# Spreading four rows of reciprocals over partitions 0, 4, 8 and 12, in an attention and MLP kernel with a planned order

## The chip, the cores and the metric

The kernel runs on one core of one Trainium2 chip. Times are device microseconds (us) of one execution; the time before is the median of three runs, 830.73 us (829.04 to 832.25). The profile is of one further execution.

A core has five engines with instruction queues of their own, which meet only through semaphores: TensorE (PE) multiplies matrices into PSUM, VectorE (DVE), ScalarE (ACT) and GpSimd (POOL) work on elements, and SyncE (SP) issues the DMA copies. Each engine takes its instructions strictly in the order in which they were written for it. Data lie in SBUF, 128 partitions wide.

## The reference

One input x of 2048 rows by 640 is normalised by row (layernorm without weights). Two branches share the result, and both are added to x:

```python
x = A_x
xn = _layernorm(x, axis=-1)
return x + _A_ref(xn, A_wq, A_wk, A_wv, A_wo) + _B_ref(xn, B_w1, B_w2)
```

Branch A is attention with 32 query heads of 20 features and a single key and value head: q = xn wq, k = xn wk, v = xn wv, softmax over 2048 keys of the scaled scores, times v, and the heads joined times wo. Branch B is silu(xn w1) w2 with 1728 hidden features. All is bf16 in and out.

## The kernel before, in words

**Tiling.** The 2048 query rows are cut in 4 chunks of 512 (QC, QW), the 32 heads in 8 groups of 4 (NG, HG), each head in a slot of 32 partitions (SLOT). That makes 32 groups (chunk, head group), in order. A group goes over 16 key tiles of 128 keys. For each key tile and head, PE makes scores of 128 keys by 512 queries in a PSUM bank (`s_mm`, line 758). Most go to ACT, two or three heads at a time, for the exponential (line 793). The others are key tiles that the planner gives to DVE, which builds the exponential of all four heads from integer and multiply steps (line 936, then 957, 959 and 961). PE then multiplies by v (lines 822 and, for the tiles of DVE, 1137) and accumulates one PSUM bank for the four heads. Row 20 of each head's slot holds the sum of the exponentials, the softmax denominator.

**End of a group.** `end_group` (line 857) copies the bank to `U_sb` (line 863). For chunks 0 to 2, which have 24 of the 32 groups, `norm_job` (line 579) then makes a chain with four SP steps:

- la (line 585): a DMA copies the four rows of denominators, 512 values each, into a [128, 16] tile.
- recip (line 588): DVE takes the reciprocals.
- lb (line 590): a DMA copies them back as four rows of 512 fp32 values to `Rrow`, which lies in partitions 0 to 3 of the middle third of `nblk`.
- lc (line 592): four DMAs, one for each head; each reads one row of `Rrow` 32 times and writes it to the 32 partitions of that head's slot in `Rrep`, 64 KB.
- normalisation (line 595): POOL multiplies `U_sb` by `Rrep` into `oU`; it waits for the four lc copies.
- packs (line 606): four or five DMAs put the heads' 20 rows each in their place in `oT`, the transposed attention output.

The last chunk normalises in another way (`ut_job`, with PE transposes).

**Other work of PE.** Between the attention steps PE projects q (line 502), makes the hidden layer (line 522, with its activation on ACT, line 528, and DVE, line 531) and the output. An output job (`out_job`, line 623) of a chunk makes 128 rows by 320 columns in one PSUM bank: 14 matmuls of branch B (`ffn_mms`, line 556) and then 5 of branch A (`o_mms`, line 561, matmul on line 565), which read `oT` and so wait for all packs of that chunk. DVE adds x (line 635), SP stores (line 620).

**What sets the order.** A planner in Python (`Sched`, `build`) runs through the program once with an estimated duration for each operation and writes one list for each engine; `emit` (line 1306) turns the dependences into semaphore waits. The chip's true times change no order. At each step the planner picks, for the engine that is free first, an operation whose estimated start is near; PE chooses among scores, PV, the current other job and DVE's key tiles. A job of the other work, once begun, is finished before the next begins (`cur_job`, line 1158), and holds one of the two spare banks (`XBANKS`, line 33 and following; DVE's key tiles use them too). For an SP operation the planner counts 600 ns of SP time and a single common DMA stream, whose time for a copy is its stated number of bytes over 250 per ns (lines 303 and 304):

```python
op = Op("sp", fn, 600.0, nbytes / 250.0, pre=pre, reads=reads, writes=writes, prio=prio, name=f"dma {key}")
```

and when the operation is put in the list (lines 204 and 205):

```python
self.dma_free = max(self.dma_free, start + 1300.0) + op.lat
op.fin = self.dma_free + 700.0
```

The stated bytes of an lc copy are `2 * SLOT * QW * 4` = 131,072, twice the 64 KB that it moves.

Of the kernel before, what the change touches and what calls it, by code (L numbers as in the profile page):

```python
# [13 lines left out]
P = 128  # L14
# [4 lines left out]
SLOT = 32  # L19
HG = 4  # L20
NG = H // HG
QW = 512
# [197 lines left out]
def build(nc, A_x, A_wq, A_wk, A_wv, A_wo, B_x, B_w1, B_w2, out, stack):  # L220
# [11 lines left out]
    def sb(shape, dt):  # L232
        cnt[0] += 1
        return stack.enter_context(nc.sbuf_tensor(f"sbt{cnt[0]}", shape, dt))

    def sem(name):
        return stack.enter_context(nc.semaphore(name))
# [27 lines left out]
    rLg = sb([P, 2, HG * QW // P], F32)  # L265
    nblk = sb([P, 3 * QW], F32)
    Rrep = nblk[:, 0:QW]
    Rrow = nblk[0:HG, QW:2 * QW]
    oU = nblk[:, 2 * QW:3 * QW].bitcast(BF16).rearrange("p (u q) -> p u q", u=2)
    o_norm = nblk[:, 0:QTP * D // 2].bitcast(BF16).rearrange("p (t d) -> p t d", t=QTP)  # L270
    t_buf = sb([P, 2, QW], BF16)
# [24 lines left out]
    def res(*k):  # L296
        if k not in R:
            R[k] = Res()
        return R[k]
# [3 lines left out]
    def dma(key, fn, nbytes, reads=(), writes=(), pre=(), prio=0.0):  # L303
        op = Op("sp", fn, 600.0, nbytes / 250.0, pre=pre, reads=reads, writes=writes, prio=prio, name=f"dma {key}")
        if key not in dma_sems:
            dma_sems[key] = [sem(f"d_{key}"), 0]
        op.dma_sem = key
        return sc.add(op)

    def dve(fn, occ, lat=65.0, **kw):  # L310
        return sc.add(Op("dve", fn, occ, lat, **kw))
# [4 lines left out]
    def pool(fn, occ, lat=60.0, **kw):  # L316
        return sc.add(Op("pool", fn, occ, lat, **kw))
# [21 lines left out]
    def load_x(n):  # L339
# [9 lines left out]
         reads=[res("idf")], writes=[res("idf")], prio=0.02)  # L349
    pool(lambda g: g.memset(mhalf[:, :], -0.5), 120, writes=[res("mh")], prio=0.03)  # L350
    idb = pool(lambda g: g.tensor_copy(ident_b[:, :], ident_f[:, :]), 290, reads=[res("idf")], writes=[res("idb")],
               prio=0.04)
    pool(lambda g: g.memset(wv_sb[:, :, :], 0.0), 180, writes=[res("wv")], prio=0.05)
    for n in range(4):
# [3 lines left out]
        writes=[res("wqp")], prio=0.06)  # L358
    vms = pool(lambda g: g.memset(v_all[:, :, :, :], 0.0), 900, writes=[res("v")], prio=0.6)
    v1s = []  # L360
    for j, cj in enumerate((1.0, C_W)):
        v1s.append(pool(lambda g, j=j, cj=cj: g.memset(v_all[:, j, :, DH:DH + 1], 0.5 * cj), 120,
                        pre=[vms], writes=[res("v")], prio=0.6 + 0.01 * j))

    def wrow(ap):
# [4 lines left out]
                writes=[res("wqs0")])  # L370
    wk_cp = [pool(lambda g, r=r: g.tensor_copy(wk_sb[:, :, r * SLOT:r * SLOT + DH], wk_sb[:, :, 0:DH]), 240, pre=[d_wk],
                  reads=[res("wk")], writes=[res("wkr", r)], prio=0.08) for r in range(1, HG)]
    for n in range(4, 8):
# [3 lines left out]
               writes=[res("wqs")])  # L377
# [3 lines left out]
    def wq_dst(c):  # L381
# [5 lines left out]
        reads=[res("wqs0")], pre=[pool_wq0, d_wq0], writes=[res("wqp0")], prio=0.15)  # L387
    wqp_op = []
    for c in range(DC):
        wqp_op.append(pool(lambda g, c=c: g.tensor_copy(  # L390
            wq_dst(c)[:, HG:H, 0:DH], wq_st[:, c, HG * DH:D].rearrange("p (h j) -> p h j", j=DH)), 640,
            reads=[res("wqs")], pre=[pool_wq0, d_wq], writes=[res("wqp", c)], prio=0.7))
# [181 lines left out]
    def oT_free(qc):  # L574
        return qc < 2 or all((qc - 2, i) in out_done for i in range(QTP))
# [3 lines left out]
    def norm_job(g, uc):  # L579

        qc, gi = divmod(g, NG)
        us, par = g % 2, qc % 2
        u0 = U_sb[DH:DH + 1, us, :]
        pu = u0.ap[0][0]
        la = dma(f"la{us}", lambda e: e.dma_start(
            Lg[:, us, :], bass.AP(U_sb, u0.offset, [[pu * SLOT, HG], [HG * QW // P, SLOT], [1, HG * QW // P]])), 8192,
            pre=[uc], reads=[res("U", us)], writes=[res("Lg", us)], prio=0.5)
        rc = dve(lambda v: v.reciprocal(rLg[:, us, :], Lg[:, us, :]), 230, pre=[la], reads=[res("Lg", us)],
                 writes=[res("rLg", us)], prio=0.1, name="recip")
        lb = dma(f"lb{us}", lambda e: e.dma_start(Rrow.rearrange("h (j e) -> h j e", j=SLOT), rLg[:, us, :]),  # L590
                 8192, pre=[rc], reads=[res("rLg", us)], writes=[res("Rrow")], prio=0.5)
        lc = [dma(f"lc{us}", lambda e, h=h: e.dma_start(Rrep[h * SLOT:(h + 1) * SLOT, :],
                                                        bass.AP(nblk, Rrow[h:h + 1, :].offset, [[Rrow.ap[0][0], 1], [0, SLOT], [1, QW]])),
                  2 * SLOT * QW * 4, pre=[lb], reads=[res("Rrow")], writes=[res("Rrep", h)], prio=0.5) for h in range(HG)]
        nm = pool(lambda e: e.tensor_tensor(oU[:, us, :], U_sb[:, us, :], Rrep, ALU.mult), 1300, pre=[uc] + lc,  # L595
                  reads=[res("U", us)] + [res("Rrep", h) for h in range(HG)], writes=[res("oU", us)], prio=0.1)
        un_op[(qc, gi)] = nm
        packs = []
        for i in range(HG):
            row = (gi * HG + i) * DH  # L600
            lo = i * SLOT
            left = DH
            while left:
                c, r = divmod(row, P)
                n = min(left, P - r)
                o = dma(f"pk{us}", lambda e, c=c, r=r, n=n, lo=lo: e.dma_start(oT[r:r + n, par, c, :], oU[lo:lo + n, us, :]),  # L606
                        n * QW * 2, pre=[nm], reads=[res("oU", us)], writes=[res("oT", par, gi, i, c)], prio=0.6)
                o.gate = lambda: oT_free(qc)
                packs.append(o)
                row, lo, left = row + n, lo + n, left - n  # L610
        pack_op[(qc, gi)] = packs
# [245 lines left out]
    def end_group(g, pv):  # L857
        us = g % 2

        def com(op):  # L860
            att["pgroup"] = g + 1
        up = [un_op[((g - 2) // NG, (g - 2) % NG)]] if g >= 2 else []
        uc = Op("dve", lambda v: v.tensor_copy(U_sb[:, us, :], bk(UB)), t_dve(512), 65, pre=[pv] + up, reads=[sc.banks[UB]],  # L863
                writes=[res("U", us)], prio=-1.0, on_commit=com, name=f"Ucopy{g}")
        sc.add(uc)
        qc = g // NG
        if qc < QC - 1:
            norm_job(g, uc)
        else:
            misc_front.append(ut_job(qc, g % NG, uc, us))  # L870
        if g == NGR - 1:
            for i in range(QTP):
                misc_front.append(("oT", qc, i))
            if qc == QC - 1:
                for i in range(QTP):
                    for hf in range(2):
                        misc_front.append(("fin", qc, i, hf))
# [391 lines left out]
    while not finished():  # L1269
# [7 lines left out]
        e = min(sc.ENG, key=lambda k: sc.t[k])  # L1277
# [127 lines left out]
def bass_kernel(nc, A_x, A_wq, A_wk, A_wv, A_wo, B_x, B_w1, B_w2, out):  # L1405
    with ExitStack() as stack:
        XB_EXTRA[:] = [b for buf in ABUFS for b in buf]
        sc, dma_sems, sem = build(nc, A_x, A_wq, A_wk, A_wv, A_wo, B_x, B_w1, B_w2, out, stack)
        run = emit(nc, sc, dma_sems, sem)
        with nc.Block() as block:  # L1410
            @block.sync
            def _(e):
                run("sp", e)

            @block.gpsimd
            def _(e):
                run("pool", e)

            @block.vector
            def _(e):  # L1420
                run("dve", e)

            @block.scalar
            def _(e):
                run("act", e)

            @block.tensor
            def _(e):
                run("pe", e)
# [34 lines left out]
```

## Time and profile before

| what | value |
|---|---|
| median of 3 runs | 830.73 us |
| the profiled execution | 830.86 us |
| its span, first to last instruction | 829.1 us |
| granted TensorE clock, mean | 0.971 |
| lc copies (line 592) | 96, 64.0 KB each, median 6.5 us from issue to landing |
| lb copies (line 590) | 24, from 57.1 to 627.7 us |
| normalisations on POOL (line 595) | 24, median 1276 ns, the first at 70.5, the last at 641.5 us |
| packs (line 606) | 108, median 716 ns of SP's time each |
| exponentials on ACT (line 793) | 651 instructions, 754.9 us busy |
| key tiles on DVE (line 961) | 105 |

How to read it: busy time of an engine is the sum of its instructions. "Idle, released by" names what an engine waited for. A landing is the time from a DMA's issue to the arrival of its last byte's semaphore. The chain is followed back from the last instruction, at each step to what released it. The clock is the one that PE was granted, as a share of full speed.

### The profile page before, as it was taken

Reading aid. Unit: us, or ns where it says so; the run is one execution under the profiler, and the core shown is the slowest. Engines: PE = TensorE matmul, PEld = TensorE weight load, DVE = VectorE, ACT = ScalarE, POOL = GpSimd, SP = SyncE. Lnnn points to the kernel's source line nnn. Section 1 sums busy time; section 2 is a strip of 40 time slices with the busy share of each in tenths; the row PEclk is TensorE's granted clock in tenths of the full one; section 3 lists DMA queues with packets and bytes.
Section 4 is the critical chain, followed back from the end, with each engine's and each line's share of the span. In section 5 each row is a group of like instructions: output and inputs, shape, how many; then the busy total and the mean of one; then the engine's idle time right before and its main releaser. Section 6 shows DMA issues by size and latency. Waiting matters only on the chain.

```text
span 829.1 us, 15373 instructions
## 1 busy us (share of the span) xinstructions
PE 734.0 (89%) x6578; PEld 237.8 (29%) x6578; DVE 665.3 (80%) x1023; ACT 771.0 (93%) x715; POOL 57.3 (7%) x64
## 2 busy tenths in 40 slices
PE   7899999988977999888896999989898799999986
PEld 5322222222222332222222333322222233333323
DVE  8468688888875897899886889899888588888773
ACT  3899999999996999999996999999999699999992
POOL 7400000000000000000000000000000000000000
PEclk9899999999997999999998999999999899999998
DMA  8403432324440444542334433433344000010000
GB/s 269 155 4 15 18 13 15 16 14 19 16 17 13 27 26 17 57 18 13 15 16 17 22 17 24 63 17 16 17 16 18 13 9 17 1 33 2 1 1 32
DMA packets 26044, 22.96 MB, mean 28 GB/s; under 512 B 11704, under 2 KB 22264, under 8 KB 25976
## 3 DMA queue, kind: packets, MB, share of 16 engines
q1 hardware_dynamic: 25976, 21.99, 30.0%
q8 instruction: 51, 0.84, 0.4%
q14 instruction: 17, 0.14, 0.1%
HBM read 10.70 MB, written 2.62 MB: 16 GB/s over the span
## 4 chain that ended last, share of the span: by engine, by line
ACT 78%; PE 10%; issue 4%; DVE 3%; DMA 2%; SPq 1%; POOL 1%; POOLq 0%
ACT sbt L793 75%; PE psall L758 3%; ACT sbt L528 3%; PE psall L556 2%; PE psall L822 2%; PE psall L565 1%; DMA sbt<-sbt 1%; DVE sbt L936 1%; SPq L606 1%; PE psall L522 1%; DMA sbt<-in_A_wq_dram 1%; PE psall L459 0%; PE psall L433 0%; DMA sbt<-in_A_wk_dram 0%; POOL sbt L595 0%
## 5 line engine op out<-in xcount | busy, mean ns | idle before, releaser
L793 ACT ACTIVATE sbt<-psall 128x1536 bf16<-128x1536 f32 (+1 forms) x651 | 754.9, 1366 | 29.5 <-PE psall L758 29.1
L936 DVE TENSOR_SCALAR sbt<-psall 128x512 int16<-128x512 f32 x420 | 282.7, 686 | 85.5 <-PE psall L758 80.9
L758 PE MATMUL psall<-sbt 32*128 32x512 bf16 x2048 | 284.4, 389 | 61.4 <-ACT sbt L793 50.4
L822 PE MATMUL psall<-sbt 128*32 128x512 bf16 x2468 | 207.0, 390 | 2.8 <-ACT sbt L793 1.5
L758 PEld LDWEIGHTS psall<-sbt 32*128 32x128 bf16 x2048 | 71.0, 91 | 296.1 <-ACT sbt L793 246.8
L961 DVE TENSOR_TENSOR sbt<-sbt 128x2048 bf16<-128x2048 bf16 x105 | 132.9, 1265 | 1.4
L556 PE MATMUL psall<-sbt 128*128 128x320 bf16 x448 | 85.5, 304 | 0.3 <-DVE sbt L936 0.2
L522 PE MATMUL psall<-sbt 128*128 128x512 bf16 (+1 forms) x280 | 81.6, 388 | 2.5 <-DVE sbt L936 1.4
L822 PEld LDWEIGHTS psall<-sbt 128*32 128x32 bf16 x2468 | 51.5, 94 | 108.5 <-issue 84.8
L959 DVE TENSOR_SCALAR sbt<-sbt 128x2048 int16<-128x2048 int16 x105 | 75.0, 715 | 1.3
L957 DVE TENSOR_SCALAR sbt<-sbt 128x2048 int16<-128x2048 int16 x105 | 73.3, 698 | 3.0 <-PE psall L822 1.4
L595 POOL TENSOR_TENSOR sbt<-sbt 128x512 bf16<-128x512 f32 x24 | 33.6, 1399 | 577.1 <-DVE sbt L936 214.9
L1137 PE MATMUL psall<-sbt 128*32 128x512 bf16 (+1 forms) x752 | 55.1, 383 | 1.2 <-DVE sbt L344 1.2
L556 PEld LDWEIGHTS psall<-sbt 128*128 128x128 bf16 x448 | 36.1, 98 | 45.0 <-issue 29.6
L565 PE MATMUL psall<-sbt 128*128 128x320 bf16 x160 | 33.0, 329 | 18.0 <-DMA sbt<-sbt 18.0
L531 DVE SCALAR_TENSOR_TENSOR sbt<-sbt,psall 128x512 bf16<-128x512 bf16 (+1 forms) x56 | 38.2, 682 | 13.0 <-ACT sbt L528 8.9
L502 PE MATMUL psall<-sbt 128*128 128x512 bf16 (+1 forms) x175 | 47.9, 370 | 0.5 <-DVE sbt L936 0.3
L528 ACT ACTIVATE sbt<-psall 128x512 bf16<-128x512 f32 (+1 forms) x56 | 43.5, 776 | 0.6 <-PE psall L522 0.6
L522 PEld LDWEIGHTS psall<-sbt 128*128 128x128 bf16 (+1 forms) x280 | 21.0, 99 | 42.2 <-issue 21.7
L863 DVE COPY sbt<-psall 128x512 f32<-128x512 f32 x32 | 21.9, 684 | 12.1 <-PE psall L822 12.0
L506 DVE TENSOR_SCALAR sbt<-psall 128x512 bf16<-128x512 f32 x32 | 21.9, 685 | 4.5 <-PE psall L502 4.0
L1137 PEld LDWEIGHTS psall<-sbt 128*32 128x32 bf16 x752 | 18.8, 102 | 19.5 <-issue 11.2
(49 smaller groups left out, 166.5 us busy)
## 6 DMA issues: line engine op xcount, KB each, us to landing
sbt<-sbt SPq DMA_DIRECT2D x96, 64.0 KB, 6.5
sbt<-in_A_x_dram SPq DMA_DIRECT2D x28, 160.0 KB, 2.9
out_dram<-sbt SPq DMA_DIRECT2D x16, 160.0 KB, 1.9
sbt<-in_B_w_dram SPq DMA_DIRECT2D x1, 2160.0 KB, 11.0
sbt<-in_B_w_dram SPq DMA_DIRECT2D x1, 2080.0 KB, 15.8
sbt<-sbt SPq DMA_DIRECT2D x84, 20.0 KB
sbt<-sbt SPq DMA_DIRECT2D x54, 8.0 KB
sbt<-in_A_wo_dram SPq DMA_DIRECT2D x1, 800.0 KB, 17.6
```

The costliest lines, as they stand in the source:

```text
L502: return pe.matmul(bk(b, lo, hi), wq_pad[:, c, g * P:(g + 1) * P], xnT[:, c, qc * QW + lo:qc * QW + hi], start=(c == 0), stop=(c == DC - 1))
L522: return pe.matmul(bk(b, 0, QW, rows=rows), w1_sb[:, c, fk * P:fk * P + rows], xnT[:, c, qc * QW:(qc + 1) * QW], start=(c == 0), stop=(c = ...
L528: t = Op("act", lambda a: a.activation(t_buf[0:rows, ts, :], bk(job.bank, 0, QW, rows=rows), AF.Tanh, scale=0.5), t_act(512), 95, pre=[job ...
L556: return pe.matmul(bk(b, 0, e1 - e0), hT[par][0:rows, fk, i * P:(i + 1) * P], w2_sb[0:rows, fk, e0:e1], start=(start and fk == 0), stop=(s ...
L758: return pe.matmul(bk(b), kT_rep[i * SLOT:(i + 1) * SLOT, kt * P:(kt + 1) * P], qT[i * SLOT:(i + 1) * SLOT, g % NQ, :], start=True, stop=T ...
L793: return a.activation(Ebuf[:, es, 0:w], ps[:, buf[0] * BANK:buf[0] * BANK + w], AF.Exp, scale=ESCALE)
L822: ins = pe.matmul(ps[i * SLOT:(i + 1) * SLOT, UB * BANK:UB * BANK + QW], lhsT, rhs, start=(first and k < HG), stop=(last and k >= len(lst) ...
L936: p1 = Op("dve", lambda v: v.tensor_scalar(z16[:, i * QW:(i + 1) * QW], bk(job.bank), ZBIAS, 0.0, ALU.add, ALU.max), t_dve(QW), 65, pre=[o ...
L957: m = dve(lambda v: v.tensor_scalar(m_t[:, :].bitcast(I16), z16, 0x7F, 0x3F80, ALU.bitwise_and, ALU.bitwise_or), t_dve(N, 4), pre=st["p1"] ...
L959: wop = dve(lambda v: v.tensor_scalar(w[:, :].bitcast(I16), z16, 0x7F80, None, ALU.bitwise_and), t_dve(N, 4), pre=[m], reads=zr, writes=[r ...
L961: zm = dve(lambda v: v.tensor_tensor(z[:, :], z[:, :], m_t[:, :], ALU.mult), t_dve(N, 2), pre=[wop], reads=zr + [res("m")], writes=zr, pri ...
L1137: ins = pe.matmul(ps[i * SLOT:(i + 1) * SLOT, UB * BANK:UB * BANK + n], zero_t[:, 0:SLOT], zero_t[:, 0:n], start=fresh, stop=fresh, tile_p ...
```

## The change

`Rrow` becomes a view of 16 partitions, of which rows 0, 4, 8 and 12 are used: lb writes its four rows there, and lc reads row 4h for head h. The stated bytes of each lc copy, which only the planner uses, go from 2 to 3 times `SLOT * QW * 4`. The number of DMAs, what they move and where it ends up in `Rrep` stay the same. The planner makes the whole order of all engines anew with the new number.

```diff
-    Rrow = nblk[0:HG, QW:2 * QW]
+    Rrow = nblk[0:4 * HG, QW:2 * QW]
...
-        lb = dma(f"lb{us}", lambda e: e.dma_start(Rrow.rearrange("h (j e) -> h j e", j=SLOT), rLg[:, us, :]),
+        lb = dma(f"lb{us}", lambda e: e.dma_start(
+            bass.AP(nblk, Rrow.offset, [[4 * Rrow.ap[0][0], HG], [HG * QW // P, SLOT], [1, HG * QW // P]]), rLg[:, us, :]),
                  8192, pre=[rc], reads=[res("rLg", us)], writes=[res("Rrow")], prio=0.5)
         lc = [dma(f"lc{us}", lambda e, h=h: e.dma_start(Rrep[h * SLOT:(h + 1) * SLOT, :],
-                                                        bass.AP(nblk, Rrow[h:h + 1, :].offset, [[Rrow.ap[0][0], 1], [0, SLOT], [1, QW]])),
-                  2 * SLOT * QW * 4, pre=[lb], reads=[res("Rrow")], writes=[res("Rrep", h)], prio=0.5) for h in range(HG)]
+                                                        bass.AP(nblk, Rrow[4 * h:4 * h + 1, :].offset, [[Rrow.ap[0][0], 1], [0, SLOT], [1, QW]])),
+                  3 * SLOT * QW * 4, pre=[lb], reads=[res("Rrow")], writes=[res("Rrep", h)], prio=0.5) for h in range(HG)]
```

## The prediction

> **What bounds the kernel now.** I read the page's busy times first, then the waits, then ACT's busy time by stretches, then the chain at the places where ACT stands still, and last the DMA traffic just ahead of them.
>
> ```profile
> PE 734.0 (89%) x6578; PEld 237.8 (29%) x6578; DVE 665.3 (80%) x1023; ACT 771.0 (93%) x715; POOL 57.3 (7%) x64
> ```
>
> ACT works 771.0 of 829.1 us, nearly all of it exponentials (line 793). Three stretches that leave out the prologue and three short places, by columns length, PE, PEld, DVE, ACT, POOL, clock, DMA share and GB/s:
>
> ```profile
> 60.00:246.00 186.00, 168.26 (x1428) 47.85 (x1424) 156.70 (x228) 185.22 (x181) 9.41 (x7) 0.99 0.37 16
> 463.00:640.00 177.00, 161.80 (x1476) 49.64 (x1479) 154.65 (x226) 176.67 (x165) 10.15 (x7) 1.00 0.42 24
> 657.40:814.00 156.60, 142.99 (x1328) 48.37 (x1326) 124.50 (x188) 155.48 (x137) 0.00 (x0) 0.99 0.03 10
> ```
>
> ACT is at 99% there. Inside these stretches only less work for ACT can help. Its idle time lies at the start and at three places, which the waits name:
>
> ```profile
> PE psall L565 <- DMA sbt<-sbt: 18.0, 3, 6.7
> ACT sbt L793 <- PE psall L758: 29.1, 19, 6.8
> ```
>
> PE stops three times, for 18.0 us together, at the o_mms matmuls (line 565) behind a DMA between SBUF addresses; ACT's longest waits for PE are at the same places. The chain at the first of them (start, length, what):
>
> ```profile
> 247.80 1.27 POOL sbt L595
> 249.09 0.80 SPq L606
> ...
> 251.47 1.90 DMA sbt<-sbt
> 253.37 0.05 issue
> 253.41 0.45 PE psall L565
> ```
>
> The normalisation of the last head group of a q chunk (POOL, line 595) starts at 247.80, four pack copies (line 606) follow, the last lands at 253.37, and PE, idle for 6.71 us since 246.70, goes on. At the other two places PE waits 5.92 us (to 452.92) and 5.41 us (to 647.16). Why does POOL start so late? It waits for the four row copies of line 592. The DMA traffic from 629 to 643 us, ahead of the third stall, in 40 slices:
>
> ```profile
> DMA  2000019999399399939939595971966111000000
> GB/s 23 0 0 0 0 12 47 41 35 29 12 35 35 12 35 29 29 12 35 35 12 47 18 29 18 47 23 6 47 23 23 29 18 47 0 0 0 0 0 0
> ```
>
> And line 592 in the group ahead of the first stall:
>
> ```profile
> DMA to landing us min/median/max: 4.6/7.3/9.3
> ```
>
> Four copies are issued within about 2.5 us (there at 236.53, 237.13, 237.77 and 238.40; ahead of the third stall from 629.84), yet traffic runs on from 631 to 641 at some 27 GB/s (4 x 64 KB in 9.7 us), with the DMA engines marked busy. The first copy lands 4.6 us after its issue, the last 9.3 us after, at 238.40 + 9.3 = 247.70; POOL starts at 247.80. So these copies go through one after the other, and they set the start of the normalisation.
>
> **The price of one stall** is more than PE's wait. The granted clock after the first stall is 0.50 until 259, and ACT idles again:
>
> ```profile
> 246.70:253.40 6.70, 0.01 (x2) 0.00 (x0) 0.00 (x0) 1.06 (x2) 1.26 (x1) 0.66 0.07 13
> 253.40:255.00 1.60, 1.59 (x8) 0.65 (x9) 0.52 (x1) 0.55 (x1) 0.00 (x0) 0.50 0.00 0
> 255.00:257.00 2.00, 2.00 (x10) 0.34 (x8) 0.67 (x2) 1.73 (x2) 0.00 (x0) 0.50 0.03 8
> 257.00:259.00 2.00, 2.00 (x9) 0.39 (x7) 0.31 (x1) 0.54 (x2) 0.00 (x0) 0.50 0.00 0
> ```
>
> From ACT's timeline: first stall 6.69 + 0.27 + 1.47 + 0.16 = 8.6 us of idle ACT; second 6.8; third 5.28 + 1.25 = 6.5. Together **21.9 us**. That is all there is to gain here.
>
> **The change, part by part.**
>
> *Number of instructions.* 24 groups, each with 1 copy lb, 4 copies lc, 1 normalisation, 4 or 5 packs, as before; SP's issue time of about 0.6 us for each stays. Nothing on PE, ACT or DVE is added. Cost 0.
>
> *lb to partitions 0, 4, 8, 12.* Same bytes in the same 64-byte pieces. From the issue of lb (234.46) to the first lc (236.53) it takes 2.07 us now; its traffic is a small part of that, so I give it 0 (at most 0.2 us either way, ten per cent of the step).
>
> *lc from four rows farther apart.* No row of this trace shows two copies from rows four partitions apart. Bounds: at worst the four still go in sequence, as now, and nothing is gained; a loss I exclude, because each copy still moves the same 32 pieces of 2 KB out of one partition. At best each lands as the first one does, 4.6 us after its issue: the last gains 9.3 - 4.6 = 4.7 us. Two rows decide between these. The output stores, which read 128 partitions of SBUF, land 160 KB in a median 1.9 us, while the row copies need a median 6.5 us for 64 KB: the engines are not what limits, the source rows are. And the first copy shows what one row alone costs. I take the near side of the best end, **4.4 us**, since each copy uses the same 16 engines and can't quite ignore its neighbours: the traffic of one copy is a quarter of 9.7, so 2.4 us; the fourth starts 1.9 us (238.40 - 236.53) after the first and ends no earlier than 1.9 + 2.4 = 4.3 us into the traffic; some 0.9 us of queueing on top makes 5.3 in place of 9.7.
>
> [...]
>
> *The planner's cost, 2 to 3 units.* In line 304 a copy then counts 196,608/250 = 786 ns in place of 524. With SP's 600 ns spacing and lines 204 and 205, the last of four ends 4324 ns after the first's start now, and 5146 ns after. So in the plan, normalisation and packs come 0.82 us later, and the planner has 0.82 us more time to put other PE work ahead of the o_mms. On the chip that is worth up to 0.8 us at each of the three places. I take 0.8; bounds 0 and about 1.1 (one round of scores and PV more, e.g. 0.61 + 0.40 us).
>
> *At the 21 other groups* the normalisation comes 4.4 us sooner, too; PE never waited for those packs, SP only holds its queue less long for line 595 (225.6 us over 24 groups). Worth 0. The out job holds one of two spare banks 0.8 us longer in the plan, one 0.69 us step of DVE (line 936) at each of three places; I count it within the range.
>
> *The sum.* Sooner and later together 4.4 + 0.8 = 5.2 us at each stall. PE's waits become 6.71 - 5.2 = 1.5, 5.92 - 5.2 = 0.7 and 5.41 - 5.2 = 0.2. ACT's idle time then is about 2.4 us, plus 1.0 us for some lowered clock after the longest: 3.4 in place of 21.9. **Gain 18.5 us.** What follows each stall is ACT at 99%, so it passes to the end whole. The profiled execution took 830.86 us (span 829.1 and 1.8 around it), 0.13 over the median 830.73. 830.86 - 18.5 = 812.4. What is late next is ACT itself.
>
> **The new order.** From the first out job on (246 of 829 us) the planner's times differ, so all it decides later may differ. Price: one key tile (four heads) that moves from DVE to ACT costs 4 x 754.9/1628 = 1.86 us of ACT (651 instructions, 326 of three tiles and 325 of two). There are 105 such tiles on DVE. I allow 4 of them either way, +-7 us.
>
> **Rivals.**
> 1. *Half the overlap*: the engines take copies partly in turn, and the last lands only 2 us sooner. PE's waits become 3.9, 3.1 and 2.6, the lowered clock stays in part (2 us in all). Gain 21.9 - 9.6 - 2 = 10 us: about 820. For it: all copies use the same engines.
> 2. *Still in sequence*: the move does nothing, the plan's 0.8 us at three places remains: 830.9 - 2.4 = 828.5. For it: 27 GB/s is also what engines in turn would show. Against it: stores of 160 KB in 1.9 us.
> 3. *Slower*: the new plan gives DVE fewer key tiles, in the part behind the first out job, because its spare banks are held longer; at 1.86 us for a tile it decides from 10 tiles (18.5 us) on, and from 13 the kernel is slower by over 0.5%: 835 or more. Against it: only three holds of 0.8 us change in the plan. For it: a greedy plan can turn on small times.
>
> **How the numbers follow.** Forecast 0.68, its own range 803 to 820; half the overlap 0.14 (816 to 824); still in sequence 0.10 (825 to 832); slower 0.08 (835 to 845). The range for 8 in 10 takes the forecast and nearly all of the half: 803 to 825. A measurement of this kernel can tell about 0.5% (4.2 us) from no change. Faster by more than that (under 826.6): 0.68 + 0.14 + a fifth of the sequence = 0.84; within it 0.08; slower 0.08.
>
> **What would show it.** Right: the four lc copies land 4.5 to 5.5 us after their issue, all alike; GB/s above 27 in bursts of some 5 us; PE's wait at line 565 for DMA under 4 us in all; no clock of 0.50 behind it; ACT at 95% or more. Wrong: landing still 9 us for the last (rival 2); or landing as forecast and ACT's count of exponentials risen from 651, its busy time well over 771 us (rival 3); or a new wait of PE in place of line 565.

## The result, and the profile after

The changed kernel takes 810.56 us (median of 4 runs, 807.85 to 810.83) against 831.49 us (4 runs, 829.04 to 836.88) for the kernel before, measured together: a ratio of 0.9732, 95% interval 0.968 to 0.9785. Forecast were 812.4 us and a range of 803 to 825. The profiled execution took 810.33 us with a span of 808.5 us; the one before 830.86 and 829.1.

In the changed file everything after line 590 stands one line lower: the exponential is line 794, the score matmul 759, PV 823, the row copies 593, POOL's normalisation 596, the packs 607. Busy times, waits, and the landing of all 96 row copies (least, median, longest) in the changed kernel:

```profile
PE 717.0 (89%) x6501; PEld 235.2 (29%) x6554; DVE 668.3 (83%) x1030; ACT 769.5 (95%) x714; POOL 58.1 (7%) x64
```

```profile
PE psall L565 <- DMA sbt<-sbt: 1.5, 2, 1.1
...
ACT sbt L794 <- PE psall L759: 11.9, 17, 1.8
```

```profile
DMA to landing us min/median/max: 3.5/3.8/4.8
```

ACT's work is nearly the same (771.0 before). What shrank is its idle time, 829.1 - 771.0 = 58.1 us before and 808.5 - 769.5 = 39.0 after. PE's waits for a DMA at line 565 fell from 18.0 to 1.5 us. The row copies land after 3.5 to 4.8 us, where it was 4.5 to 9.8. The traffic ahead of the first output job (229 to 243 us, 40 slices):

```profile
DMA  0000000100000001110001999709979671100000
GB/s 0 0 0 0 0 0 0 17 6 0 0 0 0 0 0 47 10 13 0 0 0 12 47 41 35 29 35 117 129 70 117 53 35 6 18 6 0 0 0 0
```

The same 256 KB that took some 10 us at 27 GB/s now pass in about 5 us, with slices above 100 GB/s. On the chain of waits in that place POOL starts at 241.80, and PE's matmul follows the last pack:

```profile
241.80 1.35 POOL sbt L596
...
243.17 0.79 SPq L607
...
245.54 1.90 DMA sbt<-sbt
...
247.49 1.25 PE psall L565 x4
```

From the issue of the first row copy to POOL's start it is 241.80 - 235.45 = 6.35 us; before, 247.80 - 236.53 = 11.27. The four copies of this group land 3.7 to 4.4 us after their issue, where it was 4.6 to 9.3.

### The profile page after: what moved, and what is told of

Same layout as the page of the kernel before. It is cut to its first block, busy times and chain, and to the rows that moved or that the text cites. A ratio compares the mean times of both kernels' runs of the same rounds, so it can differ in the third digit from the quotient of the medians.

```text
span 808.5 us, 15272 instructions
## 1 busy us (share of the span) xinstructions
PE 717.0 (89%) x6501; PEld 235.2 (29%) x6554; DVE 668.3 (83%) x1030; ACT 769.5 (95%) x714; POOL 58.1 (7%) x64
## 4 chain that ended last, share of the span: by engine, by line
ACT 80%; PE 13%; DVE 4%; DMA 1%; SPq 1%; issue 1%; POOL 0%; ACTq 0%
ACT sbt L794 76%; PE psall L759 4%; ACT sbt L528 3%; PE psall L556 3%; PE psall L823 2%; PE psall L565 1%; DVE sbt L937 1%; DVE sbt L960 1%; PE psall L502 1%; DMA sbt<-in_A_x_dram 1%; SPq L607 1%; DMA sbt<-sbt 0%; DVE sbt L962 0%; PE psall L459 0%; POOL sbt L596 0%
## 5 line engine op out<-in xcount | busy, mean ns | idle before, releaser
L794 ACT ACTIVATE sbt<-psall 128x1536 bf16<-128x1536 f32 (+2 forms) x650 | 754.9, 1365 | 12.6 <-PE psall L759 11.9
L937 DVE TENSOR_SCALAR sbt<-psall 128x512 int16<-128x512 f32 x424 | 286.0, 685 | 77.8 <-PE psall L759 73.6
L962 DVE TENSOR_TENSOR sbt<-sbt 128x2048 bf16<-128x2048 bf16 x106 | 129.6, 1223 | 1.2
L960 DVE TENSOR_SCALAR sbt<-sbt 128x2048 int16<-128x2048 int16 x106 | 78.3, 739 | 1.1
L958 DVE TENSOR_SCALAR sbt<-sbt 128x2048 int16<-128x2048 int16 x106 | 74.6, 703 | 3.4 <-PE psall L823 1.4
L522 PE MATMUL psall<-sbt 128*128 128x512 bf16 (+1 forms) x252 | 73.6, 383 | 4.0 <-issue 1.6
L1138 PE MATMUL psall<-sbt 128*32 128x512 bf16 (+1 forms) x724 | 53.4, 377 | 1.5 <-DVE sbt L344 1.2
L502 PE MATMUL psall<-sbt 128*128 128x512 bf16 (+1 forms) x153 | 41.0, 367 | 2.2 <-issue 1.3
L864 DVE COPY sbt<-psall 128x512 f32<-128x512 f32 x32 | 21.9, 686 | 10.4 <-PE psall L823 10.3
```

The source lines that it names most:

```text
L502: return pe.matmul(bk(b, lo, hi), wq_pad[:, c, g * P:(g + 1) * P], xnT[:, c, qc * QW + lo:qc * QW + hi], start=(c == 0), stop=(c == DC - 1))
L522: return pe.matmul(bk(b, 0, QW, rows=rows), w1_sb[:, c, fk * P:fk * P + rows], xnT[:, c, qc * QW:(qc + 1) * QW], start=(c == 0), stop=(c = ...
L794: return a.activation(Ebuf[:, es, 0:w], ps[:, buf[0] * BANK:buf[0] * BANK + w], AF.Exp, scale=ESCALE)
L937: p1 = Op("dve", lambda v: v.tensor_scalar(z16[:, i * QW:(i + 1) * QW], bk(job.bank), ZBIAS, 0.0, ALU.add, ALU.max), t_dve(QW), 65, pre=[o ...
L958: m = dve(lambda v: v.tensor_scalar(m_t[:, :].bitcast(I16), z16, 0x7F, 0x3F80, ALU.bitwise_and, ALU.bitwise_or), t_dve(N, 4), pre=st["p1"] ...
L960: wop = dve(lambda v: v.tensor_scalar(w[:, :].bitcast(I16), z16, 0x7F80, None, ALU.bitwise_and), t_dve(N, 4), pre=[m], reads=zr, writes=[r ...
```

## The experiments

Two things were changed at once: the place of the rows and the planner's count. Theory: the place makes the copies land sooner, PE's three waits at line 565 shrink, ACT goes on. Rivals: the new order of the engines is the cause; the copies still hinder each other by engine and not by place. All ratios are to the kernel before on the same chip, run beside each group of experiments (medians 832.20, 831.23 and 832.75 us on the three chips used), so they, and not the medians of different chips, are to be compared.

**The place alone.**

```diff
-                  3 * SLOT * QW * 4, pre=[lb], reads=[res("Rrow")], writes=[res("Rrep", h)], prio=0.5) for h in range(HG)]
+                  2 * SLOT * QW * 4, pre=[lb], reads=[res("Rrow")], writes=[res("Rrep", h)], prio=0.5) for h in range(HG)]
```

> Rows in partitions 0, 4, 8 and 12, the planner's count left at 2: no engine's order changes. My theory: the row copies land as in the changed kernel (about 3.8 us median, 4.8 the longest), the three PE waits at line 565 fall by about 4.9 us each, from 18.0 us to about 3.3 us together, and the time is 813 to 817 us. Rival (the gain is the planner's new order): landing as short, but the time is 822 us or more.

809.32 us, ratio 0.9725 (0.9678 to 0.9771). PE's waits for the DMA are 1.9 us in all, where 3.3 was expected, and the time is below the range expected. The planner's input is the one of before, and every engine executes as many instructions as before (PE 6578, DVE 1023, ACT 715, POOL 64), so the gain is the place's alone:

```profile
PE psall L565 <- DMA sbt<-sbt: 1.9, 2, 1.7
```

**The planner's count alone.**

```diff
-                  2 * SLOT * QW * 4, pre=[lb], reads=[res("Rrow")], writes=[res("Rrep", h)], prio=0.5) for h in range(HG)]
+                  3 * SLOT * QW * 4, pre=[lb], reads=[res("Rrow")], writes=[res("Rrep", h)], prio=0.5) for h in range(HG)]
```

> Rows left in partitions 0 to 3, the planner's count 3: the changed kernel's order with the old copies. My theory: landing as before (median 6.5 us, longest near 9.5), PE's three waits shorter by about 0.8 us each (some 15.6 us together), 826 to 830 us. Rival (the new order is what helps): 815 us or less. Rival (the new order is worse by itself and the sooner copies pay for it): over 833 us.

830.61 us, ratio 0.999 (0.9961 to 1.0019): no gain that can be told. The waits are 6.11, 5.54 and 5.31 us, shorter by 0.60, 0.38 and 0.10; in place of 2.4 us that is 1.1. ACT's waits for PE did not shrink at all (29.1 before):

```profile
ACT sbt L793 <- PE psall L758: 29.7, 23, 6.1
PE psall L565 <- DMA sbt<-sbt: 17.0, 3, 6.1
```

The rival of a worse order falls too. The two experiments together say that the change is one part that acts and one that does nothing measurable.

**The count at 7, rows left in partitions 0 to 3.**

```diff
-                  2 * SLOT * QW * 4, pre=[lb], reads=[res("Rrow")], writes=[res("Rrep", h)], prio=0.5) for h in range(HG)]
+                  7 * SLOT * QW * 4, pre=[lb], reads=[res("Rrow")], writes=[res("Rrep", h)], prio=0.5) for h in range(HG)]
```

> Rows left in partitions 0 to 3, the planner's count 7: the plan's last copy then ends 9.34 us after the first's start in place of 4.32, so 5.0 us more work is put ahead of the matmuls that wait. My theory (sooner data and later planning are worth the same at the stalls): landing as before, PE's waits under 4 us together, 809 to 817 us. Rival (only sooner copies help; work moved ahead is missing later, or the spare bank that the output job holds costs DVE key tiles): 822 us or more.

816.18 us, ratio 0.98 (0.9744 to 0.9856). The copies land as before (4.5/7.1/9.5), yet the kernel is 2% faster, within the expected 809 to 817. So the stall itself is the cost, and a later plan can shorten it too, though in this run the order of the engines changed with it. But the waits went to 7.7 us and not under 4: of three times 5.0 us planned, 10.3 us arrived.

```profile
PE psall L565 <- DMA sbt<-sbt: 7.7, 3, 3.1
```

**What do the rows share?** Three kernels with the planner's count at 2 and every list as before; only the step between the four rows differs (`Rrow` made tall enough):

```diff
-            bass.AP(nblk, Rrow.offset, [[4 * Rrow.ap[0][0], HG], [HG * QW // P, SLOT], [1, HG * QW // P]]), rLg[:, us, :]),
+            bass.AP(nblk, Rrow.offset, [[32 * Rrow.ap[0][0], HG], [HG * QW // P, SLOT], [1, HG * QW // P]]), rLg[:, us, :]),
...
-                                                        bass.AP(nblk, Rrow[4 * h:4 * h + 1, :].offset, [[Rrow.ap[0][0], 1], [0, SLOT], [1, QW]])),
+                                                        bass.AP(nblk, Rrow[32 * h:32 * h + 1, :].offset, [[Rrow.ap[0][0], 1], [0, SLOT], [1, QW]])),
```

Step 32:

> Rows in partitions 0, 32, 64 and 96, the planner's count 2, order as before. If any distance between the rows is enough: landing as with step 4 (median 3.8, longest 4.8 us), 813 to 817 us. [...]

Step 36 (36 in place of 32 in both lines):

> Rows in partitions 0, 36, 72 and 108, the planner's count 2, order as before: nearly the same distance as in the run with 0, 32, 64 and 96 (826 us, landing 4.6/5.8/8.0), but other low bits of the partition number. My theory (what rows share goes by those bits): landing and time as with 0, 4, 8 and 12: 3.6/3.8/5.1 and 808 to 812 us. Rival (the distance of 32 and more, or partitions above 32, cost it): landing near 5.8 in the median, 822 us or more.

Step 16 (16 in both lines):

> Rows in partitions 0, 16, 32 and 48, the planner's count 2, order as before. By my theory the first and third row share a path, and the second and fourth, but two copies in a row never do. If sharing is all that counts: longest landing 6 to 8 us, as with 0, 32, 64 and 96, and 820 to 827 us. If only neighbours in the queue hinder each other: median about 4 us and 810 to 816 us.

| rows in partitions | landing, least/median/longest | median time | ratio (interval) |
|---|---|---|---|
| 0, 1, 2, 3 (before) | 4.5/6.5/9.8 | 832.20 and 831.23 | 1 |
| 0, 32, 64, 96 | 4.6/5.8/8.0 | 826.29 | 0.9915 (0.9883 to 0.9946) |
| 0, 16, 32, 48 | 3.9/4.6/6.0 | 816.25 | 0.9801 (0.9763 to 0.9839) |
| 0, 36, 72, 108 | 3.6/3.8/5.3 | 808.75 | 0.9723 (0.9689 to 0.9756) |
| 0, 4, 8, 12 | 3.6/3.8/5.1 | 809.32 | 0.9725 (0.9678 to 0.9771) |

The median of before is that of the chip of rows 0, 32, 64, 96 and 0, 4, 8, 12, then that of the other two.

The pair 32 and 36 decides. Distance is the same within an eighth, and both reach above partition 95, yet by the medians one takes 17.5 us longer, and the intervals of the ratios lie far apart. Among rows 32 partitions apart some hinder each other (the longest landing is 8.0 us), and rows 36 apart do not (5.3, where rows 4 apart have 5.1). The traffic in GB/s with step 32 and then with step 36, both from 234 to 248 us in 40 slices:

```profile
GB/s 18 0 0 0 0 0 0 47 1 22 0 0 0 0 47 41 29 35 12 47 18 29 23 41 23 12 117 70 47 18 23 29 18 23 23 18 6 0 0 0
```

```profile
GB/s 23 0 0 0 0 29 41 47 18 29 53 129 123 59 111 53 29 18 12 0 0 0 0 0 0 0 0 0 59 0 59 0 53 6 29 29 0 0 0 0
```

With step 32 the traffic begins near 30 GB/s and lasts some 8 us, with one short burst of up to 117; with step 36 it is through in some 5 us, and slices reach 129 GB/s, where four rows in partitions 0 to 3 gave some 27, with no slice above 50 ahead of the three stalls. So the 27 GB/s was not the engines' limit, and distance alone does not decide. That it goes by certain bits of the partition number was my theory, and step 36 came out within its 808 to 812 us; what it is that the rows share, no run shows. Step 32 took 826.3 us, far above the 813 to 817 expected if any distance were enough. With step 16, where by my theory the rows that share are never neighbours in the queue, the time came out between the two expectations (816.3 us, median landing 4.6 us, longest 6.0). That sharers hinder each other more when they follow each other would explain it. This stays argued. No run here shows an engine's queue by itself, and the two runs differ in the rows as well as in the order. The rows of step 32 in the order 0, 64, 32, 96 would show whether the order counts; no run has it.

**One DMA for all four rows.**

```diff
-        lc = [dma(f"lc{us}", lambda e, h=h: e.dma_start(Rrep[h * SLOT:(h + 1) * SLOT, :],
-                                                        bass.AP(nblk, Rrow[4 * h:4 * h + 1, :].offset, [[Rrow.ap[0][0], 1], [0, SLOT], [1, QW]])),
-                  3 * SLOT * QW * 4, pre=[lb], reads=[res("Rrow")], writes=[res("Rrep", h)], prio=0.5) for h in range(HG)]
+        rp = Rrow.ap[0][0]
+        lc = [dma(f"lc{us}", lambda e: e.dma_start(
+            Rrep,
+            bass.AP(nblk, Rrow.offset, [[4 * rp, HG], [0, SLOT], [1, QW]])),
+            8 * SLOT * QW * 4, pre=[lb], reads=[res("Rrow")], writes=[res("Rrep", h) for h in range(HG)], prio=0.5)]
```

> Rows in partitions 0, 4, 8 and 12, and one DMA in place of the four lc copies: it reads each row 32 times and writes all 128 partitions. Three issues of about 0.6 us less for SP in each group; the planner counts the same bytes in one operation, so orders change. My theory: each row still needs about 2.4 us and the four run side by side, landing 4 to 5 us after the only issue, so POOL starts 1.5 to 2 us sooner than with four copies; 805 to 809 us. Rival (one DMA is spread over fewer engines by its shape and these become the limit): landing 8 us or more, 820 us or more.

808.25 us, ratio 0.9718 (0.9672 to 0.9764). Traffic of one group, 234 to 246 us:

```profile
DMA  0010200000222222222000000000001103011020
GB/s 0 0 55 3 25 0 0 0 0 0 96 96 102 109 89 96 96 109 75 7 0 0 0 0 0 0 0 0 0 0 38 31 0 68 0 27 41 0 68 0
```

Some 100 GB/s, by my estimate four rows at about 25 each, with a DMA share of 0.2, as much as three of the 16 engines always at work would give, and no slower for it. POOL starts 240.50 - 235.82 = 4.7 us after the issue, in place of 6.35 (the profile gives no landing for this copy). That is 1.7 us sooner in the chain, within the 1.5 to 2 expected; the time does not show it against the place alone, since little of the stalls is left.

**The count at 5 with the new place**: 5 in place of 3 in the changed kernel's line.

```diff
-                  3 * SLOT * QW * 4, pre=[lb], reads=[res("Rrow")], writes=[res("Rrep", h)], prio=0.5) for h in range(HG)]
+                  5 * SLOT * QW * 4, pre=[lb], reads=[res("Rrow")], writes=[res("Rrep", h)], prio=0.5) for h in range(HG)]
```

> Rows in partitions 0, 4, 8 and 12 and the planner's count 5: the last copy ends 7.24 us after the first's start in the plan in place of 4.32. With the place alone PE still waits 1.9 us at line 565 and ACT idles some 4 us at the three places. My theory: these waits go to about 0, and 804 to 808 us. Rival (a new order costs as much as the rest of the waits gives, as with the count alone): 808 to 813 us.

809.87 us, ratio 0.9736 (0.9699 to 0.9773). No wait for a DMA at line 565 is left in its profile. By stretches, around the first output job and in the 163 us after it:

```profile
230.00:262.00 32.00, 29.49 (x282) 9.39 (x280) 26.86 (x40) 31.80 (x29) 1.36 (x1) 1.00 0.21 18
262.00:425.00 163.00, 145.73 (x1294) 45.45 (x1305) 143.19 (x210) 160.66 (x151) 9.39 (x7) 1.00 0.19 24
```

ACT is busy for 31.80 of 32 us where the changed kernel has 28.57, but idles 2.3 us in the next stretch, where the changed kernel idles 0.2. Most of the first difference goes with the clock, 0.89 there in the first profile of the changed kernel: in its second profile (last section) the clock is 1.00 from 244 to 254 us, and ACT's waits for scores in the 32 us come to 0.20 + 0.37 + 0.17 = 0.7 us. The 2.3 us are at clock 1.00: near 283 us ACT waits 2.21 us for scores while PE works through 19 matmuls of an output job. The rival was right: this order gives back in other places what the vanished wait saved.

**Place alone and full change, side by side.** Both kernels once more, unaltered, in more rounds.

> The place alone once more, beside the full change on the same chip, in more rounds. My theory by now: the place carries the whole gain and the planner's 3 is worth nothing that can be told: both 808 to 811 us, their medians within 2 us of each other. Rival (the new order costs something, as the count alone did not gain its 2.4 us): the full change slower than the place alone by 2 us or more.

> The full change, unaltered, beside the place alone on the same chip. My theory: 808 to 811 us, within 2 us of the place alone. Rival (the planner's 3 helps by its 0.8 us at each stall): 2 us or more faster than the place alone.

808.86 us (0.9727, 0.968 to 0.9773) and 810.12 us (0.9726, 0.9686 to 0.9766). The planner's 3 is worth nothing that can be told, either way. No version tried beats the place alone by more than the runs scatter.

## Why the prediction was right, step by step

*Where the time was.* Right. The three stalls and what follows them were the reserve; from ACT's timeline its idle time at the three places is now 1.12 + 0.88 + 0.17 + 1.05 = 3.2, 0.2 and 0.7, together 4.1 us, where 3.4 was forecast and 21.9 had been.

*The row copies.* Right in kind, a little small: 4.4 us forecast, 11.27 - 6.35 = 4.9 measured. It is even past the upper bound of 4.7. The mistake was in the row that I took for one copy alone: the first copy's 4.6 us can't have been free of the copies behind it, since with the rows in partitions 0, 4, 8 and 12 all four land after 3.7 to 4.4 us. The sign I had named, 4.5 to 5.5 us, was missed on the better side. The engines, whose turns I feared, were a small obstacle at most: the traffic takes about 5 us, and 5.3 were forecast.

*lb.* 234.46 to 236.53 before, 233.55 to 235.45 after: 2.07 and 1.90 us, within the 0.2 allowed.

*The planner's shift.* Wrong, by little: 0.8 us at each stall forecast, 2.4 us in all. Alone it shortened the waits by 0.60, 0.38 and 0.10 us and the time not at all. The shift in the plan is no amount of work: the planner can put ahead only what is ready, and at the first stall that was one set of four score matmuls.

*The lowered clock.* 1.0 us allowed, and no row was behind that number. It turned out to depend on the execution (last section). The sign "no clock of 0.50 behind it" was missed in the first profile: the 3.2 us of idle ACT at the first place lie behind PE's wait, at clock 0.50. In the second profile, after the same wait at clock 1.00, ACT idles 0.37 + 0.17 = 0.5 us.

*The new order.* From the first out job on it did change: 106 key tiles on DVE in place of 105, ACT's busy time 1.5 us less. Within the +-4 tiles. At 728 to 736 us ACT idles anew, 0.82 + 1.30 + 0.26 + 1.25 = 3.6 us, at a clock near 0.5; against that stand about 5 us less idle time in small pieces (1.8 us near 340, 1.6 us in the tail behind the last exponential, the rest spread). These can't be put down to the order. In the second profile of the same program ACT idles 0.81 us near 727, and the tail is 15.1 us as before the change; the 1.8 us near 340 are gone with the place alone, too, whose order is that of before.

*The sum.* 18.5 us forecast; 830.86 - 810.33 = 20.5 in the profiled executions: 21.9 - 4.1 = 17.8 from the stalls, 1.5 from ACT's work, 5 - 3.6 = 1.4 from the small pieces, within rounding. That the sum came so near is in part luck, since its errors offset each other: the planner's 2.4 us brought nothing that can be told, the row copies gave 0.5 us more at each stall than forecast, and PE's remaining waits, 1.5 us where 2.4 were forecast, cost ACT less than their length, while the lowered clock cost more than its 1.0.

*The rivals.* Half the overlap and still in sequence fall to the landing times; slower falls to 106 key tiles. A kernel like "half the overlap" exists: with step 32 the last copy lands 1.8 us sooner than before, and the gain is about 6 us (832.2 to 826.3), less than the 10 us I had priced: its three PE waits still make 11.7 us, where I had 9.6.

## What to carry to other kernels

Several small copies that wait on each other may be bound by where their source rows lie: look for traffic that stays at one low rate over all copies (here some 27 GB/s) and for landing times that rise from copy to copy (4.6 to 9.3 us), and try several steps between the rows, since more distance is not always better: steps of 4 and 36 brought the median landing from 6.5 to 3.8 us, steps of 16 and 32 only to 4.6 and 5.8. A planner that fixes the order from estimated durations stalls where an estimate is too short; the true fix is to make the copy as fast as the plan believes, since a longer estimate alone (count 7) bought only part of it. When the last wait is gone, what remains is the busiest engine's own work, and further edits to the order only move its gaps about.

## What the runs showed of the hardware

After a PE wait of 1.10 us the clock was halved in one execution and left alone in another. The full change was profiled twice. Both executions have the same wait of 1.10 us at line 565 near 247 us. In the six us after it, the first profile and then the second (columns as before, the clock third from the end):

```profile
248.00:254.00 6.00, 5.53 (x25) 1.35 (x24) 2.89 (x5) 3.70 (x4) 0.00 (x0) 0.50 0.01 3
```

```profile
248.00:254.00 6.00, 5.47 (x38) 1.79 (x38) 3.95 (x7) 5.36 (x5) 0.00 (x0) 1.00 0.02 5
```

At clock 0.50 ACT is busy 3.70 us of six, at 1.00 it is 5.36. From 724 to 737 us the clock is 0.61 in the one and 0.89 in the other. In the first it falls near 725.4 us, and there PE had no gap longer than 0.51 us in the 20 us ahead, so no run shows that the wait of 1.10 us is what lowers the clock. The spans are 808.5 and 805.4 us. Of the six executions in the second run of this program, the three with a mean clock of 0.985 to 0.987 have spans of 805.1 to 806.3 us, the three at 0.977 have 810.8 to 811.7: part of the scatter between executions goes with the granted clock.
